# Attention loop of a gated attention + mixture-of-experts layer: values one pair later, a third buffer of exponentials, 128 columns of the exponential on VectorE and GpSimd

## The chip, the core and the metric

One core of one Trainium2 chip. The metric is device time in microseconds (us); the kernel before takes 1339.47 us (median of three runs, 1339.27 to 1339.75). Times inside an execution are counted from the start of the profiled span.

## What is computed

x has 2048 rows of 448, float32. Two branches read it and a sigmoid gate mixes them; the part that the change touches is the attention branch, 16 heads of 28.

```python
qkv = (x @ wqkv).reshape(B, S, 3, H, Dh)            # S 2048, H 16, Dh 28
p = softmax(einsum("bhqd,bhkd->bhqk", q, k) * scale)
a = einsum("bhqk,bhkd->bhqd", p, v) ... @ wo
# top 2 of 8 experts per row: silu(x @ w1[e]) @ w2[e], weighted by a softmax of two logits
out = g * a + (1 - g) * b                           # g = sigmoid((x * gate_w).sum(-1))
```

## The kernel before

The first 834 us compute projections, the routing and the experts, with the row maxima of the scores beside them. Then the attention stage runs to 1299 us, and the output projection of 16 row tiles (L1102) to the end. The attention stage and the projection are what the change touches.

The attention stage is a loop over 128 pairs `m`. A unit `u` is 4 heads by 512 queries (16 units); a pair `p` of a unit is two key tiles of 128 (8 pairs to a unit). For a pair, `scores(m)` computes 2 x 4 score blocks of 128 keys by 512 queries on TensorE in three passes (L734): the first key tile fills PSUM bank z0 and the three banks s0, the second fills s1 and z1. The exponentials of these eight blocks go to one tile `P`. ScalarE does z0 (L1185, 512 columns), s0 (L1186, 1536 columns), s1 (L1194, 1536 columns), and of the block in z1 the first 448 columns (L1195). For that block VectorE first copies the scaled score to SBUF (`X`, L1187). The last PW = 64 columns of `X` get their exponential by a polynomial, `power`, a generator whose pieces are put between other work: `u` on VectorE (L1201), `g` on VectorE (L1203), two steps of the polynomial and the exponent bits `e` on GpSimd (L1204 to L1206), three more steps on VectorE (L1209) and the product, written to `P` (L1211).

`values(m)` multiplies `P` with the values on TensorE, 288 query columns into z0 and 224 into z1 (L1225), so both banks serve scores and values in turn. VectorE adds the two parts to the accumulator `osb` of the unit (L1235; L1233 for a unit's first pair). `beside(m)` puts one small piece of other work behind each pair: the softmax sums' way through DRAM (L1114 to L1127, GpSimd's queue), the division of a finished unit (L1132), loads of keys and values (SyncE's queue), and the routed expert rows: gathers by GpSimd (L1064), sums and weights by VectorE (L1075 to L1079) into a tile `b1`, of which all 16 stay in SBUF until the projection's `finish` (L1105) adds them. `after_sum` (L1069) is a one-column GpSimd operation that lets a gather wait for the accumulator.

TensorE, VectorE, ScalarE and GpSimd run their instructions in the order in which the code is written; the order on SyncE's queue is found by a scheduler. The loop is

```python
for m in range(NU * NPR):
    if m + 1 < NU * NPR:
        scores(m + 1)
    values(m)
    ...
    beside(m)
    if m + 1 in powers:
        next(powers[m + 1])
```

Of the kernel before, what the change touches and what calls it, by code (L numbers as in the profile page):

```python
# [9 lines left out]
F32 = mybir.dt.float32  # L10
# [4 lines left out]
ALU = mybir.AluOpType  # L15
# [22 lines left out]
NT = S // 128  # L38
# [25 lines left out]
def tile_gated_mha_moe(ctx: ExitStack, tc: tile.TileContext, x, xe_, xT, wv, wqk, wo, w1, w2, out):  # L64
# [9 lines left out]
    neg_d = dram.tile([1, S], F32, name="neg_d")  # L74
    v_d = dram.tile([S, 512], F32, name="v_d")
    sum_d = dram.tile([NG * 4, 4, 512], F32, name="sum_d")
    inv_d = dram.tile([NG * 4, 4, 512], F32, name="inv_d")
# [989 lines left out]

    def after_sum(u):
        nc.gpsimd.tensor_scalar(sb.tile([128, 1], F32, name="seen"), accs[u][:, 511:512], 0.0, None, op0=ALU.add)  # L1069

    def routed(t):
        yg = ygs.pop(t)
        b1s[t] = b1 = sb.tile([128, D], F32, name="b1", bufs=NT)
        for c in range(2):
            nc.vector.tensor_tensor(yg[c][:, 0], yg[c][:, 0], yg[c][:, 1], op=ALU.add)  # L1075
            yield
        nc.vector.tensor_scalar(b1, yg[0][:, 0], coef[:, 1, t:t + 1], None, op0=ALU.mult)
        yield
        nc.vector.scalar_tensor_tensor(b1, yg[1][:, 0], coef[:, 2, t:t + 1], b1, op0=ALU.mult, op1=ALU.add)  # L1079
        yield  # L1080

    def split_o_high(t, eng):
# [65 lines left out]
    NPR = NT // 2  # L1148
    PW = 64
    CA = 288  # L1150
# [22 lines left out]
    def scores(m):  # L1173
        u, p = divmod(m, NPR)
        if p == 0 and u and u + 1 < NU:
            qs[u + 1] = load_q((u + 1) // 4, (u + 1) % 4)
        X = sb.tile([128, 512], F32, name="X")
        P = sb.tile([128, 8, 512], F32, name="P")
        z, t = [None] * 2, [None] * 2
        for i in range(2):  # L1180
            kt = 2 * p + i
            z[i], t[i] = single(i), triple(i)
            three = [t[i][:, j] for j in range(3)]
            score_passes(kt, held[u // 4][0][kt // 8], qs[u], three + [z[i]] if i else [z[i]] + three)
        nc.scalar.activation(P[:, 0], z[0], AF.Exp, scale=SCALE)  # L1185
        nc.scalar.activation(P[:, 1:4], t[0], AF.Exp, scale=SCALE)  # L1186
        nc.vector.tensor_scalar(X, z[1], SCALE * math.log2(math.e), -126.0, op0=ALU.mult, op1=ALU.max)  # L1187
        if m - 1 in powers:
            next(powers.pop(m - 1), None)
        w = PW if m + 1 < NU * NPR else 0  # L1190
        if w:
            powers[m] = power(X[:, 512 - w:], P[:, 7, 512 - w:])
            next(powers[m])
        nc.scalar.activation(P[:, 4:7], t[1], AF.Exp, scale=SCALE)  # L1194
        nc.scalar.activation(P[:, 7, 0:512 - w], X[:, 0:512 - w], AF.Exp, scale=math.log(2.0))  # L1195
        Pc[m] = [P[:, i] for i in range(8)]

    def power(x, to):
        u, g, r = (sb.tile([128, PW], F32, name=f"p{c}") for c in "ugr")
        e = sb.tile([128, PW], I32, name="pe2")  # L1200
        nc.vector.tensor_scalar(u, x, ROUND, None, op0=ALU.add)  # L1201
        yield
        nc.vector.scalar_tensor_tensor(g, u, ROUND, x, op0=ALU.subtract, op1=ALU.subtract)  # L1203
        nc.gpsimd.tensor_scalar(r, g, EXP2[5], EXP2[4], op0=ALU.mult, op1=ALU.add)  # L1204
        nc.gpsimd.tensor_tensor(r, r, g, op=ALU.mult)
        nc.gpsimd.tensor_scalar(e, u, 1.5 * 2.0 ** 23, 2.0 ** 23, op0=ALU.subtract, op1=ALU.mult)  # L1206
        yield
        for c in (3, 2, 1):
            nc.vector.scalar_tensor_tensor(r, r, EXP2[c], g, op0=ALU.add, op1=ALU.mult)  # L1209
        yield  # L1210
        nc.vector.scalar_tensor_tensor(to, r, 1.0, e.bitcast(F32), op0=ALU.add, op1=ALU.mult)  # L1211

    def values(m):
# [15 lines left out]
        for n, (po, cs) in enumerate(parts):  # L1229
            if n and m + 1 in powers:  # L1230
                next(powers[m + 1])
            if p == 0:
# [4 lines left out]
    def beside(m):  # L1237
        u, p = divmod(m, NPR)
        g, qc = divmod(u, 4)
        if qc == 3 and g + 1 < NG:  # L1240
            if p == 3:
                held[g + 1] = [load_k(g + 1, 0), None], [None, None]
            if p == 4:
                held[g + 1][1][0] = load_v(g + 1, 0)
            if p == 6:
                held[g + 1][0][1] = load_k(g + 1, 1)
# [18 lines left out]
        if p in (3, 5, 6, 7):  # L1265
            next(sums.setdefault(u, routed(u)))
        if u == NU - 1:
            if p in (0, 4):
                split_o_high(p // 4, nc.vector)
            if p in (1, 7):  # L1270
                split_o_low(p // 7)

    for m in range(NU * NPR):
        if m + 1 < NU * NPR:
            scores(m + 1)
        values(m)
        u, p = divmod(m, NPR)
        if u + 1 < NU and p in (4, 6):
            after_sum(u)
            fetch_routed(u + 1, (p - 4) // 2)  # L1280
        if u == 0 and p < 2:
            after_sum(u)
            fetch_routed(u, p)
# [9 lines left out]
    for t in range(NT):  # L1293
# [11 lines left out]
        project(pa_, *halves.pop(t))  # L1305
        finish(t, pa_, b1s.pop(t))
        if t + 4 < NT:
            split_o(t + 4, nc.scalar)
# [51 lines left out]
```

## Time and profile before

| | |
|---|---|
| median of 3 runs | 1339.47 us |
| the profiled execution | 1339.91 us, span 1338.1 us, granted TensorE clock 1.00 throughout |
| TensorE busy | 1331.1 us (99%) |
| VectorE busy | 1078.8 us (81%) |
| ScalarE busy | 840.8 us (63%); from 900 to 1280 us it is busy all the time |
| GpSimd busy | 731.7 us (55%) |
| first and last L1185 | 835.38 and 1294.21 us |
| first matmul of the projection | 1299.11 us |

A matmul's end is modelled, and the recorded duration of an operation on ScalarE or VectorE overlaps the start of the next one on the same engine: a sum of durations there is more than the time passed. So cycle times are read here from start to start, and from end to end.

### The profile page before, as it was taken

What the parts mean: (1) busy time and instruction counts of PE and PEld (TensorE: products, weight loads), DVE (VectorE), ACT (ScalarE), POOL (GpSimd) and SP (SyncE); (2) the same over time, 40 slices, a digit from 0 to 9 for tenths busy, and PEclk for the clock granted to TensorE, in tenths of its full rate; (3) what the DMA queues carried; (4) which work ended last, traced back from release to release, by engine and by line L of the source; (5) the groups of instructions that cost most, each with busy time, mean ns of one, the idle gap of its engine ahead of it and who ended that gap; (6) DMA issues with size and microseconds to landing.
All of it is one profiled execution on the core that took longest, in us unless ns stands there. A gap on an engine that the chain in (4) does not pass through costs nothing. (4 is left out here: it accounts for less than half of the span.)

```text
span 1338.1 us, 32615 instructions
## 1 busy us (share of the span) xinstructions
PE 1331.1 (99%) x12214; PEld 937.9 (70%) x12214; DVE 1078.8 (81%) x1959; ACT 840.8 (63%) x1271; POOL 731.7 (55%) x980
## 2 busy tenths in 40 slices
PE   9999999999999999999999999999999999999999
PEld 8888788788887777777777777555555555555558
DVE  5736899888898888989888786778888887888886
ACT  5325454354354344443445434999999999999981
POOL 2123765676577577775786743444454444545431
PEclk9999999999999999999999999999999999999999
DMA  9887856743552465434645312312522432252214
GB/s 359 300 273 261 297 158 194 252 134 118 164 164 81 146 211 162 124 120 151 192 147 157 96 65 70 88 53 70 143 80 78 129 101 59 70 143 73 64 46 137
DMA packets 137086, 191.66 MB, mean 143 GB/s; under 512 B 24040, under 2 KB 103436, under 8 KB 136414
## 3 DMA queue, kind: packets, MB, share of 16 engines
q1 hardware_dynamic: 124846, 160.36, 38.4%
q0 software_dynamic: 11936, 28.97, 7.2%
q8 instruction: 96, 1.57, 0.5%
q14 instruction: 64, 0.52, 0.1%
q10 hardware_dynamic: 144, 0.23, 0.1%
HBM read 139.20 MB, written 60.74 MB: 149 GB/s over the span
## 5 line engine op out<-in xcount | busy, mean ns | idle before, releaser
L144 DVE TENSOR_REDUCE mp<-pm 128x3 f32<-128x1536 f32 (+1 forms) x301 | 508.8, 1733 | 11.0 <-PE pm L123 11.0
L1225 PE MATMUL z<-P,V 128*32 128x288 f32 x4064 | 246.1, 382 | 0.3 <-ACT P L1185 0.2
L1225 PEld LDWEIGHTS z<-P,V 128*32 128x32 f32 x4064 | 111.9, 109 | 131.6 <-ACT P L1185 47.7
L805 POOL TENSOR_TENSOR w2l<-w2r,w2h 128x448 fp32r<-128x448 f32 x112 | 129.2, 1154 | 117.6 <-ACT w2h L799 90.1
L1194 ACT ACTIVATE P<-s 128x1536 f32<-128x1536 f32 x127 | 192.4, 1515 | 0.0
L1186 ACT ACTIVATE P<-s 128x1536 f32<-128x1536 f32 x127 | 190.4, 1499 | 0.0
L734 PE MATMUL s<-Q,Kh 29*128 29x512 f32 x1524 | 187.4, 441 | 0.0
L734 PE MATMUL z<-Q,Kh 29*128 29x512 f32 x508 | 184.8, 442 | 0.5 <-DVE osb L1235 0.5
L1021 ACT ACTIVATE yo<-acc 128x448 f32<-128x448 f32 x64 | 34.8, 544 | 234.5 <-PE acc L1007 221.8
L1007 PE MATMUL acc<-w2h,hh 128*128 128x448 f32 x448 | 167.6, 374 | 0.3 <-PEq L819 0.3
L1007 PE MATMUL acc<-w2h,hl 128*128 128x448 f32 x448 | 166.5, 372 | 0.0
L1007 PE MATMUL acc<-w2l,hh 128*128 128x448 f32 x448 | 166.0, 371 | 0.0
L950 ACT ACTIVATE hf<-acc 128x512 f32<-128x512 f32 (+6 forms) x154 | 74.2, 482 | 138.0 <-PE acc L946 131.0
L137 DVE TENSOR_REDUCE mp<-acc 128x1 f32<-128x512 f32 x130 | 89.5, 688 | 84.8 <-PE pm L123 82.8
L1204 POOL TENSOR_SCALAR pr<-pg 128x64 f32<-128x64 f32 x126 | 30.0, 238 | 227.8 <-DVE pg L1203 206.0
L814 POOL TENSOR_TENSOR hl<-hf,hh 128x512 fp32r<-128x512 f32 x112 | 144.8, 1293 | 1.0 <-ACT hh L953 1.0
L946 PE MATMUL acc<-xeh,w1h 128*128 128x512 f32 (+3 forms) x408 | 136.8, 339 | 0.0
L946 PE MATMUL acc<-xeh,w1l 128*128 128x512 f32 (+3 forms) x408 | 136.1, 338 | 0.0
L1235 DVE TENSOR_TENSOR osb<-z,osb 128x288 f32<-128x288 f32 x224 | 95.1, 425 | 40.9 <-PE z L1225 27.7
L773 POOL TENSOR_TENSOR w1l<-w1r,w1h 128x1024 fp32r<-128x1024 f32 (+1 forms) x49 | 90.8, 1854 | 63.3 <-ACT w1h L767 47.5
L1187 DVE TENSOR_SCALAR X<-z 128x512 f32<-128x512 f32 x127 | 87.8, 692 | 34.8 <-PE z L734 15.2
L123 PE MATMUL pm<-khg,qg 28*128 28x512 f32 x894 | 110.4, 449 | 0.9 <-DVE lo L646 0.9
(230 smaller groups left out, 3022.1 us busy)
## 6 DMA issues: line engine op xcount, KB each, us to landing
w2r<-in_w_dram SPq DMA_DIRECT2D x112, 224.0 KB
w1r<-in_w_dram SPq DMA_DIRECT2D x56, 384.0 KB
ys_d<-zero_d SPq DMA_DIRECT2D x32, 448.0 KB
ys_d<-yo SPq DMA_DIRECT2D x64, 224.0 KB
x_d<-xf SPq DMA_DIRECT2D x115, 64.0 KB
qkh_d<-hi SPq DMA_DIRECT2D x28, 256.0 KB
qkl_d<-lo SPq DMA_DIRECT2D x28, 256.0 KB
w1r<-in_w_dram SPq DMA_DIRECT2D x112, 64.0 KB
```

The source lines that it names most:

```text
L123: nc.tensor.matmul(banks[n], qgs[g, qt // 4][rw, (qt % 4) * 128:(qt % 4 + 1) * 128], kh[g, kc][rw], start=True, stop=True)
L144: nc.vector.tensor_reduce(mp[:, (o + lo) % 256:(o + lo) % 256 + hi - lo], pm[h][:, lo - 3 * h:hi - 3 * h], axis=AX.X, op=ALU.max)
L734: nc.tensor.matmul(banks[j], k[rw, ks], q[rw, c], start=i == 0, stop=i == 2)
L773: nc.gpsimd.tensor_tensor(l[:, :, half], r[:, :, half], h[:, :, half].bitcast(F32), op=ALU.subtract)
L805: nc.gpsimd.tensor_tensor(w2l, w2r, w2h.bitcast(F32), op=ALU.subtract)
L814: nc.gpsimd.tensor_tensor(hl, hf32, hh[:, 0:512].bitcast(F32), op=ALU.subtract)
L946: nc.tensor.matmul(pu[:, 0:HC], a, b[:, cs], start=i == 0, stop=i == len(mms) - 1)
L1007: nc.tensor.matmul(py[:n, 0:D], a[:, cs], b, start=i == 0, stop=i == 3 * NH - 1)
L1186: nc.scalar.activation(P[:, 1:4], t[0], AF.Exp, scale=SCALE)
L1194: nc.scalar.activation(P[:, 4:7], t[1], AF.Exp, scale=SCALE)
L1225: nc.tensor.matmul(po[32 * j:32 * j + 32, cs], v[:, kt % 8, 32 * j:32 * j + 32], P[4 * i + j][:, cs], start=i == 0, stop=i == 1)
L1235: nc.vector.tensor_tensor(accs[u][:, cs], po[:, cs], accs[u][:, cs], op=ALU.add)
```

## The change

`scores(m + 2)` now stands ahead of `values(m)`, with `scores(1)` ahead of the loop, and `P` has three buffers. PW is 128. `g` is two GpSimd operations (L1206, L1207 of the changed kernel) instead of one on VectorE, so GpSimd does five operations for a pair. The pieces of `power` are spread over two pairs: `u` in `scores(m)`, the GpSimd operations at the end of the following step, the first of the three VectorE steps between the two sums of the next values, the other two at that step's end, the product in `scores(m + 2)`. The 16 finished `b1` tiles are written to DRAM (`b_d`) and read again for the projection, with 5 buffers. `after_sum` is gone. Key loads are asked for one pair earlier (`p` 2 and 5 for 3 and 6).

```diff
+    b_d = dram.tile([S, D], F32, name="b_d")
...
-    def after_sum(u):
-        nc.gpsimd.tensor_scalar(sb.tile([128, 1], F32, name="seen"), accs[u][:, 511:512], 0.0, None, op0=ALU.add)
-
     def routed(t):
         yg = ygs.pop(t)
-        b1s[t] = b1 = sb.tile([128, D], F32, name="b1", bufs=NT)
+        b1 = sb.tile([128, D], F32, name="b1", bufs=5)
...
+        nc.sync.dma_start(b_d[t * 128:(t + 1) * 128], b1)
         yield
+
+    def fetch_b(t):
+        b1s[t] = sb.tile([128, D], F32, name="b1", bufs=5)
+        nc.sync.dma_start(b1s[t], b_d[t * 128:(t + 1) * 128])
...
-    PW = 64
+    PW = 128
...
-        P = sb.tile([128, 8, 512], F32, name="P")
+        P = sb.tile([128, 8, 512], F32, name="P", bufs=3)
...
-        if m - 1 in powers:
-            next(powers.pop(m - 1), None)
+        if m - 2 in powers:
+            next(powers.pop(m - 2), None)
...
-        nc.vector.scalar_tensor_tensor(g, u, ROUND, x, op0=ALU.subtract, op1=ALU.subtract)
+        nc.gpsimd.tensor_scalar(g, u, ROUND, None, op0=ALU.subtract)
+        nc.gpsimd.tensor_tensor(g, g, x, op=ALU.subtract)
         nc.gpsimd.tensor_scalar(r, g, EXP2[5], EXP2[4], op0=ALU.mult, op1=ALU.add)
         nc.gpsimd.tensor_tensor(r, r, g, op=ALU.mult)
         nc.gpsimd.tensor_scalar(e, u, 1.5 * 2.0 ** 23, 2.0 ** 23, op0=ALU.subtract, op1=ALU.mult)
         yield
         for c in (3, 2, 1):
             nc.vector.scalar_tensor_tensor(r, r, EXP2[c], g, op0=ALU.add, op1=ALU.mult)
-        yield
+            if c != 2:
+                yield
...
-            if n and m + 1 in powers:
-                next(powers[m + 1])
+            if n:
+                for later in (m + 2, m + 1):
+                    if later in powers:
+                        next(powers[later])
...
-            if p == 3:
+            if p == 2:
                 held[g + 1] = [load_k(g + 1, 0), None], [None, None]
...
-            if p == 6:
+            if p == 5:
                 held[g + 1][0][1] = load_k(g + 1, 1)
...
         if u == NU - 1:
+            if 1 < p < 5:
+                fetch_b(p - 2)
...
+    scores(1)
+    next(powers[1])
     for m in range(NU * NPR):
-        if m + 1 < NU * NPR:
-            scores(m + 1)
+        if m + 2 < NU * NPR:
+            scores(m + 2)
+        elif m in powers:
+            next(powers.pop(m), None)
         values(m)
...
         if u + 1 < NU and p in (4, 6):
-            after_sum(u)
             fetch_routed(u + 1, (p - 4) // 2)
...
         finish(t, pa_, b1s.pop(t))
+        if t + 3 < NT:
+            fetch_b(t + 3)
```

The instructions of VectorE for one pair in the middle of the stage, before (z numbers are PSUM tiles; the last two rows are the work beside and the polynomial's steps):

```order
L1187 TENSOR_SCALAR X<-z_13114 128x512
L1211 SCALAR_TENSOR_TENSOR P<-pr,pe_13059 128x64
L1201 TENSOR_SCALAR pu<-X 128x64
L1235 TENSOR_TENSOR osb<-z_13139,osb 128x288
L1203 SCALAR_TENSOR_TENSOR pg<-pu,X 128x64
L1235 TENSOR_TENSOR osb<-z_13140,osb 128x224
L1075 TENSOR_TENSOR yg_12647<-yg_12647 128x448
L1209 SCALAR_TENSOR_TENSOR pr<-pr,pg 128x64 x3
```

and now:

```order
L1190 TENSOR_SCALAR X<-z_13184 128x512
L1216 SCALAR_TENSOR_TENSOR P<-pr,pe_13059 128x128
L1204 TENSOR_SCALAR pu<-X 128x128
L1242 TENSOR_TENSOR osb<-z_13209,osb 128x288
L1213 SCALAR_TENSOR_TENSOR pr<-pr,pg 128x128
L1242 TENSOR_TENSOR osb<-z_13210,osb 128x224
L1073 TENSOR_TENSOR yg_12726<-yg_12726 128x448
L1213 SCALAR_TENSOR_TENSOR pr<-pr,pg 128x128 x2
```

The step between the two sums is now the first of the polynomial's three, of the pair before; two are left behind the work beside, and the copy `X` follows them.

GpSimd's instructions for two pairs that have a gather behind the first, before:

```order
L1204 TENSOR_SCALAR pr<-pg 128x64
L1205 TENSOR_TENSOR pr<-pr,pg 128x64
L1206 TENSOR_SCALAR pe_10117<-pu 128x64
L1069 TENSOR_SCALAR seen<-osb 128x1
L1064 DMA yg_10147<-ys_d,slot_i 128x896
L1204 TENSOR_SCALAR pr<-pg 128x64
L1205 TENSOR_TENSOR pr<-pr,pg 128x64
L1206 TENSOR_SCALAR pe_10189<-pu 128x64
```

and now, for one pair:

```order
L1206 TENSOR_SCALAR pg<-pu 128x128
L1207 TENSOR_TENSOR pg<-pg,X 128x128
L1208 TENSOR_SCALAR pr<-pg 128x128
L1209 TENSOR_TENSOR pr<-pr,pg 128x128
L1210 TENSOR_SCALAR pe_10163<-pu 128x128
L1065 DMA yg_10193<-ys_d,slot_i 128x896
```

Three operations of 64 columns have become five of 128, and the one-column operation is gone.

TensorE at the end of the stage, before, from the last scores to the first matmul of the projection:

```order
L734 MATMUL s_19095<-Q,Kl_16807 128x512 x3
L734 MATMUL z_19094<-Q,Kl_16807 128x512
L1225 MATMUL z_19114<-P,V_16966 32x288 x8
L1225 MATMUL z_19115<-P,V_16966 32x224 x8
L1225 MATMUL z_19137<-P,V_16966 32x288 x4
L1225 MATMUL z_19138<-P,V_16966 32x224 x4
L1225 MATMUL z_19137<-P,V_16966 32x288 x4
L1225 MATMUL z_19138<-P,V_16966 32x224 x4
L1102 MATMUL s_19182<-wo_h,oh 128x448
```

and now:

```order
L735 MATMUL s_19154<-Q,Kl_16836 128x512 x3
L735 MATMUL z_19153<-Q,Kl_16836 128x512
L1230 MATMUL z_19173<-P,V_17070 32x288 x8
L1230 MATMUL z_19174<-P,V_17070 32x224 x8
L1230 MATMUL z_19198<-P,V_17070 32x288 x8
L1230 MATMUL z_19199<-P,V_17070 32x224 x8
L1230 MATMUL z_19221<-P,V_17070 32x288 x4
L1230 MATMUL z_19222<-P,V_17070 32x224 x4
L1230 MATMUL z_19221<-P,V_17070 32x288 x4
L1230 MATMUL z_19222<-P,V_17070 32x224 x4
L1105 MATMUL s_19267<-wo_h,oh 128x448
```

Three values blocks stand behind the last scores instead of two; at the start, two scores stand ahead of the first values instead of one.

## Rows read from the trace of the kernel before

**Rows 1.** Page, the ScalarE line of the 40 slices of the span (tenths busy), and the windows view, 1000 to 1100 us: stretch, length, then busy time of TensorE, its weight load, VectorE, ScalarE and GpSimd with their instruction counts, granted clock, DMA share, GB/s.

```profile
ACT  5325454354354344443445434999999999999981
...
1000.00:1100.00 100.00, 100.00 (x1548) 52.51 (x1548) 84.00 (x275) 100.00 (x110) 50.44 (x110) 1.00 0.39 105
```

**Rows 2.** Timeline, ScalarE through one pair and into the next: start us, duration us, engine, line, operation, out<-in.

```profile
1002.83 0.66 ACT L1185 ACTIVATE P<-z 128x512 f32<-128x512 f32 x1
...
1003.33 1.51 ACT L1186 ACTIVATE P<-s 128x1536 f32<-128x1536 f32 x1
...
1004.66 1.53 ACT L1194 ACTIVATE P<-s 128x1536 f32<-128x1536 f32 x1
...
1005.99 0.65 ACT L1195 ACTIVATE P<-X 128x448 f32<-128x448 f32 x1
...
1006.46 0.67 ACT L1185 ACTIVATE P<-z 128x512 f32<-128x512 f32 x1
```

**Rows 3.** Timeline, the L1185 of three successive pairs just behind a stall.

```profile
951.83 0.60 ACT L1185 ACTIVATE P<-z 128x512 f32<-128x512 f32 x1
...
955.45 0.61 ACT L1185 ACTIVATE P<-z 128x512 f32<-128x512 f32 x1
...
959.06 0.64 ACT L1185 ACTIVATE P<-z 128x512 f32<-128x512 f32 x1
```

**Rows 4.** Timeline, TensorE in the pair of rows 2 (PEld is the weight load that heads a block; in brackets its idle time and what ended it).

```profile
1002.61 0.19 PEld L734 LDWEIGHTS s<-Q,Kh 29*128 29x128 f32 x3 [0.29 <-ACT P L1194]
...
1003.55 0.64 PEld L1225 LDWEIGHTS z<-P,V 128*32 128x32 f32 x16 [0.41 <-ACT P L1185]
...
1004.48 0.57 PEld L1225 LDWEIGHTS z<-P,V 128*32 128x32 f32 x16 [0.29 <-DVE X L1187]
...
1005.41 0.18 PEld L734 LDWEIGHTS z<-Q,Kh 29*128 29x128 f32 x1 [0.36 <-DVE pg L1203]
...
1005.98 0.39 PE L734 MATMUL z<-Q,Kl 28*128 28x512 f32 x1
```

**Rows 5.** Timeline, the first L1185 of the stage, the last one, the last values, the last exponential and the first matmul of the projection.

```profile
835.38 0.60 ACT L1185 ACTIVATE P<-z 128x512 f32<-128x512 f32 x1 [0.39 <-PE s L734]
...
1294.21 0.66 ACT L1185 ACTIVATE P<-z 128x512 f32<-128x512 f32 x1
...
1294.93 4.25 PE L1225 MATMUL z<-P,V 128*32 128x288 f32 x64
...
1297.37 0.71 ACT L1195 ACTIVATE P<-X 128x512 f32<-128x512 f32 x1
...
1299.11 0.47 PE L1102 MATMUL s<-wo_h,oh 128*128 128x448 f32 x1
```

**Rows 6.** Groups by line and shape, VectorE, 850 to 1290 us: operation, out<-in, sizes, count | busy us, mean ns of one | idle before.

```profile
L1209 DVE SCALAR_TENSOR_TENSOR pr<-pr,pg 128x64 f32<-128x64 f32 x363 | 84.0, 231 | 13.0 <-POOL pr L1205 4.3
L1187 DVE TENSOR_SCALAR X<-z 128x512 f32<-128x512 f32 x121 | 83.7, 692 | 25.3 <-PE z L734 13.9 <-PE s L734 5.2 <-issue 3.0
L1235 DVE TENSOR_TENSOR osb<-z,osb 128x288 f32<-128x288 f32 x106 | 48.5, 458 | 16.4 <-PE z L1225 4.2
...
L1211 DVE SCALAR_TENSOR_TENSOR P<-pr,pe 128x64 f32<-128x64 f32 x121 | 26.1, 215 | 0.0
...
L1201 DVE TENSOR_SCALAR pu<-X 128x64 f32<-128x64 f32 x121 | 22.8, 189 | 0.0
L1075 DVE TENSOR_TENSOR yg<-yg 128x448 f32<-128x448 f32 x31 | 21.4, 691 | 0.0
```

**Rows 7.** The same view for GpSimd, over the whole span: the three operations of the polynomial, and two operations of other sizes from other stages.

```profile
L805 POOL TENSOR_TENSOR w2l<-w2r,w2h 128x448 fp32r<-128x448 f32 x112 | 129.2, 1154 | 117.6 <-ACT w2h L799 90.1 <-PE pm L123 11.5 <-POOL hl L814 7.0
L1206 POOL TENSOR_SCALAR pe<-pu 128x64 int32<-128x64 f32 x126 | 74.5, 591 | 10.6
...
L1205 POOL TENSOR_TENSOR pr<-pr,pg 128x64 f32<-128x64 f32 x126 | 41.0, 325 | 10.5
...
L1204 POOL TENSOR_SCALAR pr<-pg 128x64 f32<-128x64 f32 x126 | 30.0, 238 | 227.8 <-DVE pg L1203 206.0 <-PE z L1225 21.8
...
L320 POOL TENSOR_SCALAR tri<-jp 128x128 bf16<-128x128 f32 x1 | 0.6, 559 | 0.0
```

**Rows 8.** Timeline, GpSimd and VectorE where their operations on the polynomial and on the routed rows meet.

```profile
1002.17 0.32 POOL L1205 TENSOR_TENSOR pr<-pr,pg 128x64 f32<-128x64 f32 x1
1002.32 0.65 DVE L1075 TENSOR_TENSOR yg<-yg 128x448 f32<-128x448 f32 x1
...
1002.57 0.71 POOL L1206 TENSOR_SCALAR pe<-pu 128x64 int32<-128x64 f32 x1
...
1006.20 0.45 POOL L1206 TENSOR_SCALAR pe<-pu 128x64 int32<-128x64 f32 x1
...
1009.54 0.33 POOL L1205 TENSOR_TENSOR pr<-pr,pg 128x64 f32<-128x64 f32 x1
1009.59 0.76 DVE L1079 SCALAR_TENSOR_TENSOR b<-yg,coef,b 128x448 f32<-128x448 f32 x1
```

**Rows 9.** Timeline, the projection: the last unit's division, the last four tiles' split, and the stores of the result on SyncE's queue.

```profile
1317.15 0.69 DVE L1132 TENSOR_TENSOR osb<-osb,rs 128x512 f32<-128x512 f32 x1 [2.94 <-DMA rs<-inv_d]
...
1320.37 15.31 SPq L1107 DMA_DIRECT2D out_dram<-b  x11
...
1323.34 1.67 ACT L1085 ACTIVATE oh<-OT 128x512 fp32r<-128x512 f32 x3 [5.63 <-DMA OT<-osb]
```

More of the change, by code (lines that the diff above doesn't have):

```diff
@@ L1278, in tile_gated_mha_moe @@
         if u + 1 < NU and p in (4, 6):
-            after_sum(u)
             fetch_routed(u + 1, (p - 4) // 2)
         if u == 0 and p < 2:
-            after_sum(u)
             fetch_routed(u, p)
```

## The prediction

> **What bounds the kernel now.** I read the slices and the windows first. From the 26th slice on ScalarE is busy without a pause, and in 1000 to 1100 us both ScalarE and TensorE show 100% [rows 1]. Neither number says which of the two is the limit: a matmul's end is modelled, and ScalarE's durations overlap. So I went to the timeline of one pair. On ScalarE the starts lie 0.50, 1.33, 1.33 and 0.47 us apart, 3.63 together [rows 2]. From the end of one L1185 (1002.83 + 0.66) to the end of the next (1006.46 + 0.67) it is 3.64.
>
> The pairs behind a stall tell more [rows 3]. There L1185 starts 3.62 and 3.61 us after the one before, faster than in the steady run, but its duration grows, 0.60, 0.61, 0.64, so that the ends still lie 3.63 and 3.64 apart. ScalarE can be handed work faster; it does not finish a pair faster. The 0.66 of the steady run is 0.60 and a queue of 0.06. **ScalarE's own work of 3.63 us a pair is the limit.**
>
> Right beside it lies a loop over bank z0 [rows 4]. L1185 ends at 1003.49 and the values start at 1003.55; the next scores start at 1005.41, their third pass into z0 at 1005.98, the next L1185 at 1006.46. That is 2.97 us from an end to a start: with L1185 at 0.66 the loop takes 3.63, with 0.60 it takes 3.57. The loop follows ScalarE and has 0.06 to spare. A second loop goes over s1: L1194 ends, 0.06 later the second key tile's scores start (1002.61), 0.94 later the values. From L1185 over L1194 (0.50 + 1.33 + 1.53, without the queue 1.47) and this way to the L1185 after the next it is 3.30 + 0.06 + 0.94 + 1.86 + 0.57 + 0.48 = 7.21 for two pairs, 3.60 for one. This is a ceiling, since the 0.94 ends in a wait for L1185.
>
> The mean over the stage is (1294.21 - 835.38) / 126 = 3.6415 us [rows 5], 0.01 above the steady 3.63: a few interruptions.
>
> **ScalarE's part.** The last exponential falls from 448 to 384 columns. Its price: L1186 and L1194 (1536 columns) take 1.33 to the next start, L1185 (512) takes 0.50 [rows 2], 0.81 ns a column, so 52 ns for 64. Bounds: L1195 against L1185 gives 30 ns for 64 columns (0.50 - 0.47), and L1195's whole 0.65 per 448 columns gives 93. I take 52, since it comes from like operations. ScalarE then needs 3.58.
>
> **The order of scores and values.** Both loops stay: z0 still goes from the scores through L1185 to the values, whichever pair's values they are. What the values gain is that `P` is long finished, but they did not wait for `P`; they waited for z0 [rows 4]. So the new order by itself gives nothing to the pace. The new period lies between 3.58 (ScalarE) and 3.60 (second loop); I take 3.59, and 3.60 with the same interruptions. That is 126 x (3.6415 - 3.60) = **5.2 us less**; bounds 7.1 (at 3.585) and 2.7 (at 3.62).
>
> **The end of the stage.** After the last L1185 two values blocks followed; now three do, because two scores precede the first values. Before: 4.90 us from the last L1185 to the projection [rows 5]. Of that 0.66 + 0.06 + 2 x 1.86 = 4.44 are work, the rest is the wait for the last exponential, which ends 3.87 behind L1185 (1297.37 + 0.71). Now 0.60 + 0.06 + 3 x 1.86 = 6.24 and no wait: 1.3 more. Values behind values need no change to scores, which the 1.86 contain, so I take **1.2 us more**, bounds 0.9 and 1.4. At the start nothing is won: the second L1185 waits for ScalarE.
>
> **VectorE.** One operation less (L1203, 215 ns) and 64 columns more in five. From 64 to 448 columns a two-input operation goes from 215 to 691 ns [rows 6], 0.08 us for 64 columns. Ahead of the first sum the product and `u` grow by 0.08 and 0.03 to 0.08; that sum is idle 16.4 us over 106 ahead of it, 0.15 each, and the two use this up. Behind the second sum two steps of 0.31 replace three of 0.23, 0.07 less ahead of `X`. VectorE goes from 84% of 3.63 [rows 1], 3.05, to about 3.2 of 3.59, 89%. Cost nothing, unless GpSimd holds it up (below).
>
> **GpSimd.** A two-input operation costs 325 ns at 64 columns and 1154 at 448 [rows 7], so 463 at 128. A one-input operation is 238 at 64; the only one of 128 columns, with another output type, took 559. I take 300. For the exponent bits the bounds are 0.45 (the shortest at 64 columns [rows 8]) and 1.18 (twice the mean); I take 0.75, near the lower because the long ones are waits (next part). With 0.08 between operations [rows 8] the chain is 2 x 0.30 + 2 x 0.463 + 0.75 + 0.33 = 2.6. The rest of GpSimd's work is 50.44% of 3.63, less 1.15 for the three old ones and 0.06 for L1069: 0.62. Together 3.2 of 3.59: it fits. The upper ends give 4.2, which doesn't. The results are wanted a whole pair later, so a late chain alone costs nothing.
>
> **Where the two meet.** L1206 takes 0.71 beside L1075 and 0.45 without it; L1079, started 0.05 us into an L1205, takes 0.76, L1075 started 0.15 into one 0.65 [rows 8]. They hold each other up by 0.1 to 0.26 us. Two operations of 0.46 now lie where one of 0.33 lay. In the pairs with routed rows this may eat the 0.07 won ahead of `X`.
>
> The Trainium skill, "SBUF — State Buffer", section "Who interferes with whom", goes further: GpSimd and a VectorE operation with two SBUF inputs share a port pair, held for a whole instruction, and the other one blocks fully. By that rule the sum would be the one of the fourth rival; the rows disagree, since L1075 overlapped the last 0.17 us of an L1205 and was no longer than usual.
>
> **Routed rows through DRAM.** Sixteen stores and sixteen loads on SyncE's queue. The store waits for L1079, and what is queued behind it (Q, keys) is wanted a pair or more later: nothing. In the projection a load is asked for three tiles ahead, between stores that go out every 1.39 us (15.31 / 11) [rows 9]. The same stretch carries the last division: VectorE waits 2.94 us for its transfer and ScalarE 5.63 for the rows behind it. More traffic can push these; 0 to 2 us, I take 0.2. Loads of keys and `after_sum`: nothing.
>
> **Sum**, against the profiled execution (1339.91 us, 0.44 above the median): -5.2 + 1.2 + 0.2 = -3.8, so 1336.1, and 1335.7 against the median. Its own range is 1333 to 1338.5.
>
> **Rivals.**
> 1. VectorE late: GpSimd's longer operations push `X`, and with it values part two, by 0.03 us a pair on the mean. For it: the weight load of that part waits for `X` already [rows 4]. 126 x 0.03 = 3.8 back: 1339.5.
> 2. The loop over z0 is the limit and not ScalarE. For it: in the steady run L1185 always follows z0's third pass at the same 0.48. Against it: rows 3. Then only the longer end remains: 1340.8.
> 3. **Slower:** GpSimd becomes the bound. It decides where chain and DMA work pass 3.59 us. Between that and 4.2, at 3.8, it is 126 x 0.16 + 1.4 = 21.6 more: 1361.
> 4. **Slower:** operations with two inputs on VectorE and all of GpSimd's exclude each other for their whole length. VectorE: four of 0.31, 0.22, and 0.69 in five of eight pairs, 1.9; with GpSimd's 2.3 it is 4.2 a pair, 126 x 0.56 + 1.4 = 72 more: 1411. Before, the same sum was 2.9 of 3.63 and could not show.
>
> **Chances.** Forecast 0.60, rivals 0.11, 0.10, 0.11, 0.05, anything else 0.03. A measurement here tells 0.2% (2.7 us) from no change. Below 1336.8 lie most of the forecast: 0.50 faster. Within lie its rest and rivals 1 and 2: 0.31. Slower are rivals 3 and 4 and the rest: 0.19. The range takes in the forecast and rivals 1 and 2: 1332.5 to 1341.5.
>
> **What would show it.** Right: L1188 every 3.59 us with a duration near 0.60, the third pass of z0 0.48 ahead of it, 6.1 us from the last L1188 to the projection, GpSimd near 90% busy in the stage. Wrong: a period of 3.63 or more; VectorE's L1213 waiting for GpSimd; values part two waiting for `X` by more than now; the projection broken by a wait at its thirteenth tile.

## The result, and the profile after

| | before | changed | ratio (95%) |
|---|---|---|---|
| median, first timing, us | 1339.56 (1339.27 to 1340.56, 6 runs) | 1351.28 (1348.23 to 1351.83, 6 runs) | 1.0083 (1.0072 to 1.0095) |
| median, later, on the chip of run e17 (below), us | 1339.64 (19 runs) | 1342.93 (1341.44 to 1344.55, 10 runs) | 1.0025 (1.0016 to 1.0035) |

The changed kernel is slower, by 11.7 us in the first timing and by 3.3 us in the later one. Why there are two answers is the main finding. Which chip the first timing used is not known; "on record" below means its profile.

One profiled execution stands against one (1339.91 before, 1350.49 after, 1344.25 in e17), cut at three instructions of the timeline. The first row is called the stage below:

| us | before | predicted | changed | changed, e17 |
|---|---|---|---|---|
| first to last exponential of z0 (L1185, now L1188) | 458.83 | 453.6 | 465.48 | 458.11 |
| from there to the first projection matmul | 4.90 | 6.1 | 7.03 | 7.01 |
| from there to the end of the span | 38.99 | 39.2 | 40.72 | 41.66 |

The windows view of the changed kernel, with columns as in [rows 1]:

```profile
835.00:839.60 4.60, 3.36 (x44) 1.79 (x36) 0.92 (x2) 4.21 (x7) 1.81 (x5) 1.00 0.49 155
839.60:843.20 3.60, 3.60 (x40) 1.47 (x36) 1.58 (x4) 3.13 (x4) 2.57 (x6) 0.54 0.00 0
...
1000.00:1100.00 100.00, 99.11 (x1533) 52.88 (x1528) 90.24 (x247) 98.62 (x110) 86.48 (x157) 1.00 0.39 108
```

In 1000 to 1100 us ScalarE is no longer without a pause (98.62), and GpSimd's 86.48 and VectorE's 90.24 are near the forecast 90% and 89%. At the start of the stage TensorE pauses (3.36 busy of 4.60), and in the 3.6 us behind it the granted clock is 0.54 on the mean: nearly all of this stretch runs at the lower of the two levels, 1.2 and not 2.4 GHz.

The timeline of ScalarE, its L1188 alone, in two places (answers to [rows 2, 3, 5]):

```profile
835.47 0.60 ACT L1188 ACTIVATE P<-z 128x512 f32<-128x512 f32 x1 [0.39 <-DMA V<-v_d]
839.03 0.61 ACT L1188 ACTIVATE P<-z 128x512 f32<-128x512 f32 x1
844.22 0.60 ACT L1188 ACTIVATE P<-z 128x512 f32<-128x512 f32 x1 [1.48 <-PE s L735]
...
1160.51 0.60 ACT L1188 ACTIVATE P<-z 128x512 f32<-128x512 f32 x1
1164.19 0.60 ACT L1188 ACTIVATE P<-z 128x512 f32<-128x512 f32 x1
1168.18 0.60 ACT L1188 ACTIVATE P<-z 128x512 f32<-128x512 f32 x1 [0.31 <-ACT P L1198]
```

The duration is 0.60, the floor that [rows 3] show, so ScalarE is not the limit. The median distance is 3.596, as forecast (3.59 to 3.60). But one pair at the start takes 5.19, one in every unit 4.04 (median of 14; here 3.99, from 1164.19 to 1168.18), and one 3.78.

The timeline of VectorE and GpSimd through that long pair:

```profile
1161.29 0.69 DVE L1190 TENSOR_SCALAR X<-z 128x512 f32<-128x512 f32 x1
...
1162.10 0.22 DVE L1204 TENSOR_SCALAR pu<-X 128x128 f32<-128x128 f32 x1
1162.62 0.46 DVE L1242 TENSOR_TENSOR osb<-z,osb 128x288 f32<-128x288 f32 x1 [0.31 <-PE z L1230]
1163.00 0.28 DVE L1213 SCALAR_TENSOR_TENSOR pr<-pr,pg 128x128 f32<-128x128 f32 x1
1163.50 0.39 DVE L1242 TENSOR_TENSOR osb<-z,osb 128x224 f32<-128x224 f32 x1 [0.23 <-PE z L1230]
1163.81 0.93 DVE L1077 SCALAR_TENSOR_TENSOR b<-yg,coef,b 128x448 f32<-128x448 f32 x1
1164.67 0.92 DVE L1213 SCALAR_TENSOR_TENSOR pr<-pr,pg 128x128 f32<-128x128 f32 x2
1165.51 0.68 DVE L1190 TENSOR_SCALAR X<-z 128x512 f32<-128x512 f32 x1
...
1166.24 0.54 PEld L1230 LDWEIGHTS z<-P,V 128*32 128x32 f32 x16 [0.75 <-DVE X L1190]
...
1162.01 1.12 POOL L1065 DMA_INDIRECT yg<-ys_d,slot_i  x1 [0.16 <-issue]
1163.15 0.57 POOL L1206 TENSOR_SCALAR pg<-pu 128x128 f32<-128x128 f32 x1
1163.80 0.46 POOL L1207 TENSOR_TENSOR pg<-pg,X 128x128 f32<-128x128 f32 x1
1164.35 0.55 POOL L1208 TENSOR_SCALAR pr<-pg 128x128 f32<-128x128 f32 x1
```

`X` starts 1.32 behind its L1188 (1165.51 less 1164.19) where 0.89 is usual. Ahead of it lie two sums that wait for TensorE while GpSimd works on a gather (L1065), then L1077 at 0.93 and two steps at 0.92 together. Behind `X` the second part's values wait 0.75 for its bank (the PEld row); the next scores into z0 and so the next L1188 come late by this. The groups by line, 850 to 1290 us, show the lengthening on the mean (answers to [rows 6, 7]; L1213 was 231 at 64 columns):

```profile
L1213 DVE SCALAR_TENSOR_TENSOR pr<-pr,pg 128x128 f32<-128x128 f32 x358 | 131.2, 366 | 4.1
L1208 POOL TENSOR_SCALAR pr<-pg 128x128 f32<-128x128 f32 x120 | 51.6, 430 | 10.5
L1077 DVE SCALAR_TENSOR_TENSOR b<-yg,coef,b 128x448 f32<-128x448 f32 x15 | 13.9, 927 | 0.0
```

The end of the stage and of the program, from the timeline (answers to [rows 5, 9]):

```profile
1301.62 3.69 PE L1230 MATMUL z<-P,V 128*32 128x288 f32 x62
1305.55 2.50 PE L1230 MATMUL z<-P,V 128*32 128x224 f32 x34 [0.24 <-DVE P L1216]
...
1342.86 0.68 DVE L1108 SCALAR_TENSOR_TENSOR b<-z,coef,b 128x448 f32<-128x448 f32 x1 [1.22 <-DMA b<-b_d]
1344.93 0.45 DVE L1108 SCALAR_TENSOR_TENSOR b<-z,coef,b 128x224 f32<-128x224 f32 x1 [1.39 <-DMA b<-b_d]
```

The second last values block waits for VectorE's product L1216, and the last projection tiles wait for their routed rows from DRAM.

### The profile page after: what moved, and what is told of

It reads as the page before. It is cut to its first block, busy times and chain, and to the rows that moved or that the text cites. A ratio compares the mean times of both kernels' runs of the same rounds, so it can differ in the third digit from the quotient of the medians.

```text
span 1348.7 us, 32618 instructions
## 1 busy us (share of the span) xinstructions
PE 1335.4 (99%) x12214; PEld 944.7 (70%) x12214; DVE 1107.8 (82%) x1833; ACT 838.9 (62%) x1271; POOL 905.3 (67%) x1200
## 5 line engine op out<-in xcount | busy, mean ns | idle before, releaser
L1230 PE MATMUL z<-P,V 128*32 128x288 f32 x4064 | 252.0, 383 | 4.8 <-DVE X L1190 3.2
L1197 ACT ACTIVATE P<-s 128x1536 f32<-128x1536 f32 x127 | 185.8, 1463 | 0.0
L735 PE MATMUL s<-Q,Kh 29*128 29x512 f32 x1524 | 183.3, 433 | 1.2 <-ACT P L1189 0.8
L1189 ACT ACTIVATE P<-s 128x1536 f32<-128x1536 f32 x127 | 184.0, 1449 | 0.0
L735 PE MATMUL z<-Q,Kh 29*128 29x512 f32 x508 | 181.6, 435 | 0.1
L1213 DVE SCALAR_TENSOR_TENSOR pr<-pr,pg 128x128 f32<-128x128 f32 x378 | 138.2, 366 | 4.4
```

The costliest lines, as they stand in the source:

```text
L735: nc.tensor.matmul(banks[j], k[rw, ks], q[rw, c], start=i == 0, stop=i == 2)
L1230: nc.tensor.matmul(po[32 * j:32 * j + 32, cs], v[:, kt % 8, 32 * j:32 * j + 32], P[4 * i + j][:, cs], start=i == 0, stop=i == 1)
```

## The experiments

The edits are against the changed kernel unless said otherwise. e1 to e8 ran on one chip, e9 to e12 on a second, e13 to e16 on a third, e17 and e18 on a fourth, in this order of time. The kernel before takes 1339.3 to 1339.9 on each.

**e1, no two-input operation on GpSimd.**

```diff
-nc.gpsimd.tensor_tensor(g, g, x, op=ALU.subtract)
+nc.gpsimd.tensor_scalar(w, Xs[0][:, 0:288], 0.5, None, op0=ALU.mult)
 ...
-nc.gpsimd.tensor_tensor(r, r, g, op=ALU.mult)
+nc.gpsimd.tensor_scalar(w, Xs[0][:, 0:288], 0.25, None, op0=ALU.mult)
```

> Both two-input operations of GpSimd's chain (L1207, L1209) are replaced by one-input operations on 288 columns into a scratch tile, so that GpSimd stays as long busy but runs no operation with two SBUF inputs (the polynomial's values are left out by this). Theory A (a VectorE operation with two SBUF inputs is held until a GpSimd operation with two SBUF inputs ends): the steps L1213 fall from 366 ns to 0.28 to 0.30, the last routed operation L1077 from 927 to about 680 ns, the long pairs (3.78 and 4.04 us before the second and third pair of a unit) shrink below 3.70, the stretch from first to last L1188 falls from 465.5 to 456 to 460 us, the time from 1351 to 1341 to 1346. Theory B (GpSimd is too long busy, 86%, and its results come late): no change, 1350 to 1353. Theory C (VectorE has too many columns of its own in the routed pairs): within 2 us of 1351.

1425.59 us. My size was wrong: 288 columns took 0.96 and 1.05 us, not 0.46, and GpSimd became the bound (94.93 busy of 100, median pair 4.13). As a test of the time it failed. The durations, from the groups by line, still speak:

```profile
L1216 DVE SCALAR_TENSOR_TENSOR pr<-pr,pg 128x128 f32<-128x128 f32 x309 | 92.6, 300 | 76.9 <-POOL pr L1211 73.2
L1077 DVE SCALAR_TENSOR_TENSOR b<-yg,coef,b 128x448 f32<-128x448 f32 x13 | 8.8, 681 | 0.0
```

Beside one-input operations alone, with GpSimd busier than ever, steps take 300 and not 366, L1077 681 and not 927.

**e2, g on VectorE.**

```diff
-nc.gpsimd.tensor_scalar(g, u, ROUND, None, op0=ALU.subtract)
-nc.gpsimd.tensor_tensor(g, g, x, op=ALU.subtract)
+nc.vector.scalar_tensor_tensor(g, u, ROUND, x, op0=ALU.subtract, op1=ALU.subtract)
```

> The difference g comes back to VectorE as one operation of 128 columns; GpSimd loses a one-input and a two-input operation, 0.56 + 0.48 us a pair. Theory A: the lock keeps only L1209 as a cause; the steps fall to about 0.31, 0.17 us less a pair, and 0.28 is added, so the time stays within 4 us of 1351. Theory B: GpSimd falls from 86% to about 60%, the long pairs vanish, 1340 to 1344. Theory C: VectorE gets 0.28 us more in the three routed pairs of each of 16 units, up to 13 us more, 1358 to 1364.

1346.13 us, 1.0043 of before (1.0026 to 1.0059). Stage 459.98. The steps stay at 365, and now GpSimd's two-input operation is held too, 712 ns where it needs 0.46. Neither A's steps of 0.31 nor B's 1340 to 1344 came; C, with 1358 or more, falls.

**e3, routed operations spread out.**

```diff
-if p in (3, 5, 6, 7):
+if p in (1, 3, 5, 7):
     next(sums.setdefault(u, routed(u)))
```

> The four routed operations of a unit go to its pairs 1, 3, 5, 7 instead of 3, 5, 6, 7; nothing else changes. Theories A and C (VectorE's work per pair exceeds the period in consecutive routed pairs, and the lateness adds up): the excess of 0.2, 0.05 and 0.45 us behind pairs 5, 6 and 7 falls to 0 to 0.25 in sum, so 7 to 11 us less, 1340 to 1344. Theory B: GpSimd's work does not change, 1350 to 1353. The 1.5 us pair at the start of the stage, the end of the stage and the projection stay as they are in all theories.

1354.39 us, slower. The 3.78 pair went, as expected, but the 4.04 pair became 4.26 (median of 14). So the lateness does not add up over routed pairs; one pair is long by itself, the one whose sums meet a gather. The 1340 to 1344 of A and C fell here. But L1077 lies in that pair in both kernels, so this run does not tell the gather from L1077's hold-up.

**e4, the order alone** (e2's edit, and `PW = 64`).

> The changed kernel with 64 columns and the difference g on VectorE as before: what is left of the change is the order (values two pairs behind, three buffers for exponentials, steps two and one) and the routed rows in DRAM. If the order by itself gives nothing (ScalarE's 3.63 us a pair still set the pace): the pace is that of the kernel before, and the start (1.6), the longer end of the stage (2.1) and the projection (1.7) come on top, 1343 to 1346. If the order itself makes the long pairs: L1188's distances of 3.8 to 4.0 stay, 1348 to 1352. If the loop over z0 had been the limit and the order loosens it: below 1340.

1343.74 us, 1.0030 (1.0020 to 1.0040). Stage 458.11 against 458.83, median pair 3.633: the order by itself gives nothing to the pace, as the prediction had it. The end costs 48.2 us from the last L1188 where it was 43.9.

**e5, the gather inside the chain.**

```diff
 nc.gpsimd.tensor_tensor(g, g, x, op=ALU.subtract)
+if gathers:
+    fetch_routed(*gathers.pop(0))
 ...
-fetch_routed(u + 1, (p - 4) // 2)
+gathers.append((u + 1, (p - 4) // 2))
```

> The changed kernel with one thing moved: GpSimd issues each gather of routed rows (L1065, 1.06 us) not behind the whole polynomial chain but between its second and third operation, which puts it between the second sum of one pair and the first sum of the next. Theory D (while GpSimd works on a gather, the sums on VectorE that wait for TensorE start late: 0.60 to 0.95 us behind the last values matmul where it is 0.38 without a gather; together with L1077 and the held steps this makes the 4.04 us pairs): the release comes back to 0.38 in all units, the pairs of 4.04 us fall to 3.6 to 3.75, the stretch from first to last L1188 from 465.5 to 457 to 460, the time to 1343 to 1347. Theory A alone (only the lock of GpSimd's and VectorE's two-input operations): the pairs of 4.04 stay above 3.9, the time stays within 2 of 1351, since the chain is as long as before.

1344.51 us, 1.0037 (1.0022 to 1.0052). Stage 458.83; the pair that took 4.04 takes 3.59. The unaltered stage on this chip (e7) takes 466.51, or 465.0 without the 1.5 us that the fall of the clock costs at its start and e5 did not have: the move is worth 6.2 us. Theory D held in its price; in its detail not everywhere, since 22 parts of the values still end under a gather and are released 0.55 us after the start of their last matmul (median; 0.42 without a gather). What is left, from the waits view of VectorE, 850 to 1290 us (waited for: us, times, longest), is the chain that now ends later:

```profile
DVE pr L1216 <- POOL pr L1212: 8.3, 27, 1.0
```

**e6, eight matmuls in the pauses at the start.**

```diff
+for _ in range((5, 3)[i] if m == 2 else 0):
+    nc.tensor.matmul(z[i], held[0][1][0][:, 0], Pc[0][0], start=True, stop=True)
```

> Eight matmuls whose results are overwritten are put into the two pauses of TensorE at the start of the stage (1.34 and 0.76 us, while the second pair's exponentials run). If the fall of the granted clock to 0.54 behind these pauses costs the 5.18 us pair: the clock stays at 1.00 there, the pair takes about 3.6, the time falls by 1.5 to 1349.5 and the runs lie closer together than 1348.2 to 1351.8. If the pair is long for another reason (it is the first that waits for values): it stays at 5 us or more.

1355.59 us. The clock stayed at 1.00, but the matmuls were too long: the first two pairs took 6.22 and 6.38. Inconclusive; e13 repeats it with less.

**e7, loads ahead of the stores**, six buffers `b1` instead of five.

```diff
-finish(t, pa_, b1s.pop(t))
 if t + 3 < NT:
     fetch_b(t + 3)
+finish(t, pa_, b1s.pop(t))
```

> In the projection the load of the routed rows of tile t + 3 is issued ahead of the store of tile t, and six buffers instead of five hold them. If the loads behind the stores make the last tiles late (VectorE waits 0.28, 1.22 and 1.39 us for them): these waits vanish, from the last projection matmul to the end it is 3.5 us as before instead of 4.62, the time falls by 1.1 to 1350. If the DMA engines' own pace is the limit: no change within 0.3 in this stretch.

1351.76 us, no gain. The end behind the last matmul fell from 4.62 to 3.52, but VectorE waited 6.13 instead of 2.51 for the last division's transfer, and TensorE stood still for 1.31 ahead of the thirteenth tile: the place that the prediction had named.

**e8, combined** (edits of e2, e6, e7; the gather behind L1208's like; no polynomial for the last two pairs) and **e12, the same without e6's matmuls.**

> The difference g on VectorE as in the second experiment (1346.1), the gather issued behind the chain's first operation, the matmuls in the pauses at the start, the loads ahead of the stores, and no polynomial for the last two pairs. If the parts add up: from 1346.1 less 4 to 5 (the 1.9, 0.4 and 2.7 us of excess in the pairs with a gather), less 1.5 (start), less 1.1 to 1.9 (projection), less 0.8 (last product) gives 1337 to 1339, at or just below the kernel before; if the gather is not what makes the long pairs there, 1341 to 1343.

> The eighth experiment without the matmuls in the pauses at the start (these took 6.22 and 6.38 us for two pairs, 5.5 more than 3.57 twice). If the granted clock falls at the start as in the changed kernel, 1.6 of this is lost again: 1341.9; if it doesn't, 1340.3. The runs spread over both.

1345.79 and 1341.90 us (1.0050 and 1.0015). e12's stage is 455.24, 3.6 below the kernel before; its projection has e7's stall and one more (39.42 from first to last matmul, 35.45 in the kernel before and 36.10 in the changed one). Without the polynomial of the last pairs the end of the stage takes 6.25.

**e9, the kernel before with the routed rows in DRAM**, nothing else of the change.

> The kernel before with one part of the change alone: the routed rows go through DRAM (sixteen stores, sixteen loads, five buffers). If the loads are what makes the projection longer: 1.1 to 2.5 us from the first projection matmul to the end (38.99 before, 40.7 to 41.6 in the kernels with the whole change), the rest as before, 1340.9 to 1342.3. If the longer projection comes from the shifted stage end (its divisions and transfers meet the projection at another time): within 0.4 of 1339.7.

1341.94 us, 1.0017 (1.0008 to 1.0027). Stage and end of stage as before; the last matmul to the end takes 5.91 instead of 3.54. Waits of VectorE behind the stage:

```profile
DVE b L1111 <- DMA b<-b_d: 4.0, 3, 1.6
```

**e10, the kernel before with 96 columns.**

> The kernel before with one part of the change alone, as far as two buffers leave room: 96 columns instead of 64. ScalarE's work falls by 26 ns to 3.605 us a pair, at most 126 x 0.026 = 3.3 us less, 1336.4. VectorE gets 0.04 us in each of six operations, 0.24 a pair, from 84% to about 91%. If VectorE still keeps up in the routed pairs: 1336 to 1338. If the sums and X come late there, as in the changed kernel: 1339 to 1345.

1345.66 us, 1.0046 (1.0030 to 1.0063), median pair 3.669. Waits of VectorE, 850 to 1290 us:

```profile
DVE osb L1235 <- PE z L1225: 23.8, 105, 0.4
DVE pr L1209 <- POOL pr L1205: 13.9, 50, 0.3
```

In the old order VectorE waits for GpSimd's longer operations within the same pair (before 4.3 us in 23 waits). So 96 columns alone lose in the old order. How much of the loss is this wait, and how much the delay under gathers (table at e17), which this run shows too, is not separated.

**e11, e5 without two-input operations on GpSimd** (each replaced by one with one input of 128 columns).

> The fifth experiment (1344.5) with both two-input operations of GpSimd's chain replaced by one-input operations of the same 128 columns (0.30 instead of 0.46 us; the polynomial's values are left out by this). Theory A with a price: with nothing on GpSimd to hold VectorE's steps, L1214's like (the steps) take 0.28 to 0.30 throughout, the excess of 0.05 to 0.1 us in the routed pairs goes, the stretch from first to last L1188 falls from 458.8 to 454 to 456 and the time to 1340 to 1342. If the lock costs nothing once the gather is out of the way: within 1.5 of 1344.5, the steps shorter all the same.

1345.65 us. The steps take 310 on the mean, as A says, and the time does not fall. The stage, 461.16, holds the 5.17 pair at the start; less 1.5 for that it is 0.8 above e5's, on another chip. But the replacing operations took 0.53 each at the least and not the 0.30 expected, so GpSimd stayed as busy (89.77 of 100 in 1000 to 1100 us, 89.20 in e5). The hold-up is real; that its removal is worth nothing with a chain no longer than before is not shown.

**e13, two matmuls in the pauses, and e18, the same again.**

```diff
+if m == 2:
+    nc.tensor.matmul(z[i][:, 0:512 - 256 * i], held[0][1][0][:, 0], Pc[0][0][:, 0:512 - 256 * i], start=True, stop=True)
```

> The changed kernel with one matmul in each of the two pauses of TensorE at the start (512 and 256 columns; their results are overwritten), where the sixth experiment had eight. If the fall of the clock makes the 5.18 us pair: clock 1.00 there and the pair at 3.6 to 3.7, 1.5 us less, 1349.5, and the slowest and fastest run closer than the 3.6 us of the changed kernel. If two matmuls are not enough to keep the clock: 5.2 as before, 1351.

1342.87 us, 6.6 less than expected. The windows view shows the clock held:

```profile
835.00:839.60 4.60, 4.58 (x48) 2.27 (x40) 0.92 (x2) 4.28 (x6) 1.95 (x5) 1.00 0.55 178
839.60:843.20 3.60, 3.60 (x60) 2.00 (x56) 2.46 (x7) 3.58 (x5) 2.40 (x6) 1.00 0.02 5
```

The pair takes 3.73, not 5.19, so the lower clock is worth 1.5 us. The other 6.6 us were not explained by this edit: the long pairs were gone, with the gathers at the same place in GpSimd's order.

**e14, rows loaded early** (nine tiles into a free buffer of exponentials; the last tile's rows not sent away).

> The changed kernel with the routed rows of tiles 3 to 13 loaded before the projection, nine of them into the buffer of exponentials that comes free behind the third last pair; the last tile's rows stay where they were computed. If loads beside stores make the end longer: from the first projection matmul to the end 39 to 39.5 us as in the kernel before instead of 40.7, the time 1.2 to 1.7 less, 1349.7. If the last division is late for another reason: 40.5 or more.

1343.57 us, on the same chip as e13; the stage is 456.22, though the edit touches only loads and stores there. The clock held at the start without any filler. No L1117 waits for a load, yet the projection has two pauses of TensorE, 0.91 in its third tile and 0.52 ahead of its thirteenth, so its 41.93 to the end are no less than 40.7. The expectation failed: VectorE now waits 8.1 us for the divisions' transfers (2.9 before), so what the loads no longer cost at the end they cost there.

**e15, all of it, and e16, without the two matmuls.**

> g on VectorE, the gather behind the chain's first operation, no polynomial for the last two pairs, the matmuls of e13 and the loads of e14. From e12's stage (455.2 us from first to last L1188) and a tail of 6.25 + 39.2: 835 + 455.2 + 45.5 + 1.8 = 1337.5, 2 us below the kernel before; 1339 if the end is as in the changed kernel.

> The fifteenth experiment without the two matmuls at the start: 1337.5 in runs in which the clock holds, 1339 where it falls; on the median 0 to 1.5 more than the fifteenth.

1337.02 us (1336.13 to 1337.23) and 1338.43 us (1336.63 to 1339.80); ratios to before 0.9983 (0.9974 to 0.9992) and 0.9992 (0.9983 to 1.0001). e15 lies below both kernels, by 2.3 us below the one before. The two matmuls alone give 1.4 us and bring the spread to a third. e15's stage, 453.57, is the forecast 453.6. Both ran on a chip without the delay under gathers (e17); no run shows what they take on one with it.

**e17, the changed kernel unaltered, and e18 (e13 again) on one chip.**

> The changed kernel once more, unaltered, beside the thirteenth. If the delay of the sums under a gather depends on the chip: on a chip that has it, 1350 to 1352 with 0.53 to 0.96 us from the last values matmul to the release; on one that has it not, 1343 to 1345 with 0.38 to 0.45, and the thirteenth kernel alike. If it depends on the program: 1350 to 1352 on any chip.

> The thirteenth kernel once more. If the delay depends on the chip: the same delay or its absence as the seventeenth run beside it, and 0 to 1.6 us less time (1349.5 or 1342.5 to 1343). If it depends on the program: 1342 to 1344 whatever the seventeenth shows.

1342.93 and 1342.67 us: both without the long pairs. So the program alone does not decide it. The same pair as above, timeline of VectorE, GpSimd and ScalarE in e17:

```profile
1157.36 0.46 DVE L1242 TENSOR_TENSOR osb<-z,osb 128x288 f32<-128x288 f32 x1
1158.15 0.39 DVE L1242 TENSOR_TENSOR osb<-z,osb 128x224 f32<-128x224 f32 x1
1158.45 0.68 DVE L1077 SCALAR_TENSOR_TENSOR b<-yg,coef,b 128x448 f32<-128x448 f32 x1
...
1157.40 1.07 POOL L1065 DMA_INDIRECT yg<-ys_d,slot_i  x1 [0.16 <-issue]
...
1159.04 0.61 ACT L1188 ACTIVATE P<-z 128x512 f32<-128x512 f32 x1
...
1162.70 0.60 ACT L1188 ACTIVATE P<-z 128x512 f32<-128x512 f32 x1
```

Here the gather starts behind the first sum and covers the wait for the second, which is not late. It does not lie as in the pair above, so this pair alone proves little. In other pairs it lies alike in both runs. Timeline of one such pair, the kernel on record:

```profile
1095.52 1.06 POOL L1065 DMA_INDIRECT yg<-ys_d,slot_i  x1 [0.16 <-issue]
1095.75 0.54 PEld L1230 LDWEIGHTS z<-P,V 128*32 128x32 f32 x16 [0.32 <-DVE X L1190]
1096.12 0.46 DVE L1242 TENSOR_TENSOR osb<-z,osb 128x288 f32<-128x288 f32 x1
1097.03 0.39 DVE L1242 TENSOR_TENSOR osb<-z,osb 128x224 f32<-128x224 f32 x1 [0.25 <-PE z L1230]
```

and e17:

```profile
1091.92 1.06 POOL L1065 DMA_INDIRECT yg<-ys_d,slot_i  x1 [0.16 <-issue]
1092.15 0.54 PEld L1230 LDWEIGHTS z<-P,V 128*32 128x32 f32 x16 [0.33 <-DVE X L1190]
1092.43 0.46 DVE L1242 TENSOR_TENSOR osb<-z,osb 128x288 f32<-128x288 f32 x1
1093.21 0.39 DVE L1242 TENSOR_TENSOR osb<-z,osb 128x224 f32<-128x224 f32 x1
```

In both, TensorE's weight load for the second part starts 0.23 behind the gather. The first sum starts 0.60 behind the gather on record and 0.51 in e17, the second 1.51 and 1.29. The wait view of VectorE, 850 to 1290 us, first the kernel on record:

```profile
DVE osb L1242 <- PE z L1230: 12.3, 46, 0.6
```

and e17:

```profile
DVE osb L1242 <- PE z L1230: 0.9, 4, 0.3
```

From the matmuls and the semaphore events of the traces, for each part of the values: the time from the start of its last recorded matmul to the signal that releases VectorE's sum, in us, least to most (with a gather, the median ahead of that) and the count, by whether GpSimd worked on a gather in that time:

```
                 no gather             a gather
before           0.37 to 0.45 (222)    0.45; 0.35 to 0.61 (32, and one at 1.16)
on record        0.37 to 0.48 (194)    0.63; 0.45 to 0.99 (61)
e7               0.37 to 0.47 (195)    0.65; 0.45 to 1.30 (60)
e10              0.37 to 0.45 (222)    0.77; 0.46 to 0.90 (33)
e13              0.37 to 0.48 (208)    0.42; 0.38 to 0.45 (47)
e17              0.37 to 0.47 (211)    0.42; 0.42 to 0.45 (43, and one at 1.31)
```

So the same stage is delayed on the chip of e7 and not on that of e17. The undelayed runs are also the later ones, and no chip was timed both with and without the delay: whether it belongs to the chip or to something else that differed between the timings is not separated.

## Why the prediction was wrong, step by step

It said 1335.7 us and "faster"; it was 1351.28, outside the range. The profiled executions differ by +10.6 where -3.8 was forecast. On the chip of e17, too, the 1342.93 us lie above the range.

- **ScalarE and the pace: right.** Without disturbance a pair takes 3.59, and L1188 lasts 0.60. That the order "by itself gives nothing to the pace" is shown by e4. That 64 more columns lower the median distance from 3.633 (e4) to 3.596 also answers rival 2: ScalarE's work had set the pace.
- **"Cost nothing": the step that failed most.** I weighed GpSimd's work as a load that fits or doesn't (rival 3) and never asked where in the pair its gather would then lie. From the start of its first operation to the end of its last, GpSimd's chain for a pair grew from 1.41 to 2.93 us (medians; 2.6 forecast, but L1206 takes 0.54 and not 0.30). Before, a gather starts 1.4 us ahead of the next sum; behind the longer chain 0.6. On record, a sum whose wait a gather overlaps is mostly released 0.1 to 0.3 us late, and with L1077 and the steps behind it `X` is late too. TensorE's weight loads wait longer for `X` than before, the sign that the prediction had named (waits view, 850 to 1290 us, before and on record):

```profile
PEld z L1225 <- DVE X L1187: 29.8, 105, 0.4
PEld z L1230 <- DVE X L1190: 43.6, 114, 0.8
```

  The same kernel without the delay has a stage 7.4 us shorter (465.48 against 458.11), most of it in two distances of each unit: on the median 4.04 against 3.66 and 3.78 against 3.66, the others within 0.08. Moving the gather took 6.2 back on a chip that has the delay (e5 against e7). That the delay is the cause of all 7.4 is argued from these two. The trace of before held a hint: 33 parts end under the tail of a gather, 14 of them released later than 0.5.
- **"Where the two meet": mechanism seen, size wrong.** I allowed 0.1 to 0.26 us and the 0.07 ahead of `X`. A step that starts during GpSimd's two-input operation L1209 takes 0.52 instead of 0.28. The Trainium skill, "SBUF — State Buffer", section "Who interferes with whom", says that the one that comes second is blocked for the other's whole instruction; the trace on record agrees for GpSimd's two-input operations (69 steps that started 0.09 into an L1209 ended 0.146 to 0.151 behind it), not for its one-input L1206 (75 steps that started during one took 0.28, the median). My reading of one row against it in [rows 8] was too little. Its price in time was not 72 us (rival 4): the sums and `X`, which read PSUM, last as long as before (0.46 and 0.69). No run isolates the price. Without the gather's delay it is at most what is left of the stage in e17, 458.11 - 1.5 - 453.6 = 3.0; with it, the hold-up lengthens L1077 too (0.93, 0.69 in e17), and its share in the 7.4 is not known.
- **"At the start nothing is won": a loss missed.** Two scores ahead of the first values make TensorE pause for 1.34 and 0.76 us; the granted clock in the 3.6 us behind that is 0.54, 1.5 us lost (e13; e15 against e16: 1.4). In e4, e5, e12 and e14 the clock held without a filler, and the pair was not long.
- **The end of the stage: 6.1 forecast, 7.03.** "No wait" was wrong: with late steps L1216 comes late for the second last values, and TensorE idles 0.24 ahead of them. Without the polynomial of the last two pairs it is 6.25 (e12, e15, e16).
- **"I take 0.2" for the rows in DRAM: 2.0** (e9, 1341.94 less 1339.94), the upper bound. I compared the rate of stores with the loads' place in the queue, not the time until a load lands: VectorE waits three times, 4.0 us in all. That the loads are late because they wait for a buffer and land beside stores is argued; in e7, with six buffers and the loads first, this wait fell from 2.9 to 0.9 and the division's grew.

Summed: 7.4 (gather) + 1.5 (clock) + 3.0 (rest of the stage) + 0.9 (end) + 1.5 (projection here) = 14.3 of the distance of 14.4. The sum closes by construction, since the 3.0 is a remainder. In e17 the 7.4 falls away and the projection is 2.5 above the forecast: 1.5 + 3.0 + 0.9 + 2.5 = 7.9. The rival nearest to it was the first, VectorE late and `X` pushed, at a price of 3.8 instead of 10; it blamed the length of GpSimd's operations and not the place of the gather.

What stays open: what differs between the chips, or between the timings. The gather itself takes 1.03 to 1.18 us on record and 1.03 to 1.08 in e17. Which signals are delayed, and whether the matmul's end or its signal is late, the trace does not tell.

## What to carry to other kernels

When work moves to an engine that also issues transfers, ask where in the period those transfers will then lie and what runs under them, not only whether the engine has room. Deepening a pipeline is paid at both its ends: a pause at the start that lowers the clock, a block more at the end. Before a difference of under 1% is explained, time the same kernel a second time, on another chip.

## What was not expected of the hardware

- While GpSimd works on an indirect gather, the sum on VectorE that waits for TensorE is released late in the kernel on record, e2, e3, e6, e7 and e10: 0.62 to 0.77 us (the median of each run) after the start of the last matmul, against 0.42 without a gather. In e13 to e18, on two other chips, it is 0.38 to 0.45 with a gather too, but for one case.
- GpSimd's one-input operation with one arithmetic step takes 0.53 us at 128 columns (L1206; e11) and 0.92 to 1.05 at 288 (e1's L1210); with two steps and a float32 result it takes 0.30 at 128 when nothing holds it (L1208, the shortest).
- A pause of 2.1 us in TensorE, in two pieces, was followed by 3.4 us at the lower clock in some executions (the kernel on record, e1, e2, e3, e7, e11, e16, e17) and by none in others (e4, e5, e12, e14).
